# A branch for rare slots moved to the program's end, record reads freed of the scatters, and weights of the second layer requested from the last slot

## The chip, the core and the metric

The kernel runs on one core of a Trainium2 chip. Its time is device microseconds of one execution. TensorE (PE in the profile) does the matrix products, VectorE (DVE), ScalarE (ACT) and GpSimd (POOL) the element work, and SyncE (SP) issues most of the transfers. POOL issues the indirect transfers, which read or write rows by a list of indices. Each engine works through its own list of instructions in order, and waits for the others by semaphores.

## The reference

Three stages follow one another over 8 sequences of 576 tokens, 4608 tokens of 512 values in all:

```python
ret = scores * Dmat            # retention: causal, decaying, 8 heads of 64
x = (ret @ v)                  # 4608 x 512
logits = x @ w_gate + modality_bias[modality_id]
e_idx = argmax(logits); gate_w = softmax(logits)[e_idx]
out[mask] = gate_w[mask] * (relu(x[mask] @ w1[e]) @ w2[e])   # 8 experts, 512 -> 1024 -> 512
h = x @ w_in                   # second layer: 512 -> 2048
out = (relu(h) ** 2) @ w_out   # 2048 -> 512
```

Everything is fp32. Which expert a token goes to is known only when the kernel runs.

## The kernel before

**Retention and routing (0 to about 180 us).** 36 tiles of 128 tokens are computed by PE. The routing of a group of tiles gives every token a row in a table `perm`, sorted by expert. POOL writes these rows by indirect transfers (`perm<-gt,pi`, L467), one for 128 tokens, each with a small `spacer` instruction ahead of it (L464), which holds the transfer back until a given instruction of ACT, DVE or PE has run.

**The experts (about 180 to 611 us).** The sorted tokens are cut into slots of 512, each with the weights of one expert. Slot 0 is worked in two halves of 256 rows, slots 1 to 7 in two halves of 256 to 512 columns, and slot 8 has 384. For a half of slot 0, SP reads its records from `perm` (`records_rows`, L556), POOL turns the row numbers into integers (`rixr`, L558) and gathers the tokens by two indirect transfers (`xg<-xl,rixr`, L565). ACT and DVE copy them (`xn`, L571), PE transposes them (`tr`, L581) and multiplies: `hp` (first product, L615 to L617), `hh` and `hl` (the activated result on ACT and DVE, L620 and L621), `yp` (second product, L640). For the later slots the gather (`xg<-xl,rix`, L549) takes eight transfers a half, and DVE transposes (L597). Every fp32 operand is split into a high and a low part, so that a product is three matmuls. `craw`, `ca`, `cm` and `cw` (L802 to L825) prepare the weights of the second layer meanwhile: an integer addition on POOL (L807), two chains on ACT and DVE, and a transfer to memory.

**The order of this work is written out by hand.** The dictionary `OPT` holds for each slot the tick at which a step is put into the engines' lists: `e0` for slot 0 (`rec` the reading of the records, `g1` the gather of the second half, `xn1` its copies, `raw` the weight loads), `bs` for the later slots. Its entry `m2` gives the steps for the second layer that the last slot's ticks hold: `wl` requests a block of input weights (`wq_load`, `wqr<-cw`, L1037), `ws` forms its sums on POOL (`wq_sums`, L1043), `wh` splits it on ACT and DVE (`wq_split`), `xf`, `xs`, `xh` and `xp` do the like for the tokens, `ol` and `oh` for the output weights (`wor`). A framework adds the waits: by default a read of `perm` waits for every earlier write to it, and every later write waits for the read.

**Rare slots.** 9 slots always run (`NSURE`). Up to 7 more run if the experts' shares of the tokens need them: `with tc.If(st.hv > 0)` at L1336, between the last slot and the second layer. On these inputs it isn't taken; all engines then jump over its body.

**The second layer (about 611 to 1388 us).** 72 pairs `hquad(n)` (42 matmuls: seven products of the first layer for one block, `px`, `py` and `pr_all`, L1368 to L1370) and `zquad(n)` (24 matmuls of the second, `zp`, L1427 to L1430). PE's list has hquad 0, hquad 1, zquad 0, hquad 2, zquad 1 and so on. Between a quad's products ACT copies them out of PSUM into `mc` (L1378, L1381, L1385), POOL adds (L1382 to L1387), DVE adds and squares (L1390, L1391), ACT and DVE make the high and low parts `gh` (L1394) and `gl` (L1395) for the zquad. `mc` has one buffer. The lists `before`, `gaps`, `posts` and `tails` set at which quad the next weights and tokens are loaded and split. At the end POOL writes the rows of the result by indirect transfers (`out<-zo,ti`, L1444).

Of the kernel before, what the change touches and what calls it, by code (L numbers as in the profile page):

```python
# [77 lines left out]
def consts():  # L78
# [28 lines left out]
    sm[:, 228] = p // Q  # L107
    c["csta"] = np.concatenate([tri, gj, tabk.reshape(P, -1), tabs.reshape(P, -1)], 1).astype(np.float32)
# [16 lines left out]
OPT = dict(manual=True, nbig=10,nlate=10,nx=2,b0=2,bl='SG',rl=2,pz=5,ve=lambda m:'GV' if m<3 or m%4==0 else 'GS',vn=(4,4,2),egn=2,nps=2,npo=1,npt=2,npm=4,nwarm=11,ew=(20,25,32,33),es={23:1,24:1,25:1,26:1,28:1,29:1,30:1,31:1},rlag=1,rlagl=1,rlate=35,rperl=30,e5=5,e6=4,ld=4,rper=8,nw=3,biasat=4,keep=(5,0,4,2),nxw=3,scs=2,e3=13,ylag=2,zlag=2,gb=3,zb=4,cf=(0,6,7,12),cf0=(0,8,9,13),hv=10,zend=1,cwm={0:3},cws={i:(1 if i<4 else 2) for i in range(2,14)},cv0=8,scat=lambda i,n: 2,f3=33,f4=34,f5=34,e0=dict(ro=1,esplit={2:4,3:2,4:2},r1=0,r2=2,r3=2,tab=(7,8,8,9),rec=5,raw=(0,0,1,3),g1=7,split={5:2,6:2,7:2,8:3,9:3,10:2,11:2},xn1=11,tr0=6,tr1=4),hh=3,hl=3,ylag2=1,bs1=dict(regs=1,rec=1,raw=(3,4,5,6),g0=3,g1=7,gn0=(2,)*4,gn1=(2,)*4,split={6:1,7:1,8:2,9:2,10:1,11:2,12:2,13:1,14:2,15:2},tr0=10,tr1=13,cv=1),bs=dict(regs=-9,rec=-9,raw=(0,3,6,8),g0=-4,g1=4,gn0=(1,)*8,gn1=(1,)*8,split={3:1,4:2,6:1,7:1,8:2,9:3,10:2,11:1,12:2,14:1},tr0=5,tr1=13,cv=2,f0=7,p0=13,m2={1:('wl 0','xf'),4:('ws 0','xs 0'),5:('xh 0',),6:('wh 0 0',),7:('xs 1',),8:('xh 1',),9:('wh 0 1','wl 1','xs 2'),10:('xh 2','xp 1','ol 0'),11:('xp 4','ws 1'),12:('wh 1 0',),13:('wh 1 1',),14:('oh 0',),15:('oh 1',)}))  # L125


def kernel_body(tc, I, out):
# [90 lines left out]
    pq = small[:, 228:229]  # L219
    modi = cp.tile([P, NTILE, 2], I32, name="mod_c")  # L220
# [167 lines left out]
    st.fine = True  # L388

# [62 lines left out]
    def route3(gi):  # L452
# [5 lines left out]
        for i in range(n):  # L458
            def f(i=i):
# [9 lines left out]
                tc.add_to_no_dep_group("scat", sc.ins)  # L469
            soon.append((gi, f))  # L470
# [58 lines left out]

    def records(row, n):  # L530

        rec = sp.tile([P, 2, 8, 2], F32, name="rec", bufs=3)
        src = perm[ds(row, n * HW)].rearrange("(h i a) w -> h i (a w)", h=n, a=8)
        for h in range(n):
            nc.sync.dma_start(out=rec[:, h].rearrange("p a w -> p (a w)"), in_=bc(src[h], 0, 4))
        return rec
# [1005 lines left out]
```

## Time and profile before

| what | value |
|---|---|
| time, median of 3 runs | 1398.53 us (1396.82 to 1400.24) |
| profiled execution | 1399.43 us, its span 1397.6 us |
| PE busy | 1354.1 us, 97% of the span |
| DVE, POOL, ACT busy | 871.6, 537.2 and 519.4 us |
| granted TensorE clock, mean | 0.990 |
| transfers | 182.08 MB, mean 130 GB/s |

The profile shows one execution. A bracket behind an instruction is the time for which its engine stood idle ahead of it, and what it waited for last. [...] Busy shares over the whole span hide where PE stands: it has to be looked for stretch by stretch.

### The profile page before, as it was taken

How to read it: one execution, taken by the hardware profiler on the slowest of the kernel's cores; microseconds unless marked ns; L12 is line 12 of the kernel's file. 1: busy time of each engine (PE TensorE's matmuls, PEld its weight loads, DVE VectorE, ACT ScalarE, POOL GpSimd, SP SyncE). 2: the span in 40 equal slices, each digit the busy share in tenths (PEclk: the TensorE clock that was granted, in tenths of full speed). 3: DMA queues.
4: the chain of work that ended last, by engine and by line, in shares of the span. 5: the costliest groups of instructions: out<-in, count | busy, mean ns of one | idle time of the engine just before them, and what ended most of it. 6: DMA issues, size and time to landing. Idle time of an engine off the chain costs nothing.

```text
span 1397.6 us, 24821 instructions
## 1 busy us (share of the span) xinstructions
PE 1354.1 (97%) x9728; PEld 1187.9 (85%) x9728; DVE 871.6 (62%) x1320; ACT 519.4 (37%) x969; POOL 537.2 (38%) x675
## 2 busy tenths in 40 slices
PE   9999997999999999989999999999999999999996
PEld 7877787878888888988989989988988998998895
DVE  6667776698777877647455445454666655656542
ACT  2323353354443444334333333333433333333321
POOL 0123455454453535134322222235733344244332
PEclk9999998999999999999999999999999999999998
DMA  8799877467765667431111100113222222122210
GB/s 295 220 234 235 235 176 251 154 198 226 245 225 188 205 211 251 122 102 37 61 61 61 61 31 31 61 61 106 83 84 61 91 91 77 45 81 72 91 62 30
DMA packets 99243, 182.08 MB, mean 130 GB/s; under 512 B 25004, under 2 KB 43820, under 8 KB 94764
## 3 DMA queue, kind: packets, MB, share of 16 engines
q1 hardware_dynamic: 90412, 160.95, 37.9%
q0 software_dynamic: 8704, 19.45, 4.4%
q8 instruction: 78, 1.28, 0.4%
q14 instruction: 49, 0.40, 0.1%
HBM read 133.58 MB, written 46.77 MB: 129 GB/s over the span
## 4 chain that ended last, share of the span: by engine, by line
PE 53%; issue 1%; DMA 0%; POOL 0%; DVE 0%; SPq 0%; ACT 0%; POOLq 0%; DVEq 0%
PE zp L1428 9%; PE zp L1427 9%; PE zp L1430 9%; PE px L1370 5%; PE px L1369 5%; PE px L1368 5%; PE py L1368 2%; PE py L1370 2%; PE py L1369 2%; PE pr_all L1370 1%; PE pr_all L1368 1%; PE pr_all L1369 1%; DMA yraw<-yT 0%; POOL out L1444 0%; DVE wql L1017 0%
## 5 line engine op out<-in xcount | busy, mean ns | idle before, releaser
L1427 PE MATMUL zp<-woh,gh 128*128 128x512 f32 x576 | 227.9, 396 | 0.0
L1428 PE MATMUL zp<-wol,gh 128*128 128x512 f32 x576 | 227.5, 395 | 0.0
L1382 POOL TENSOR_TENSOR mc<-mc 128x256 f32<-128x256 f32 x72 | 56.3, 782 | 432.9 <-ACT mc L1381 432.8
L1390 DVE TENSOR_TENSOR mc<-px,mc 128x512 f32<-128x512 f32 x72 | 49.8, 691 | 260.8 <-POOL mc L1386 260.7
L549 POOL DMA_INDIRECT xg<-xl,rix x136 | 143.7, 1057 | 168.2 <-DVE rix L542 130.1
L1430 PE MATMUL zp<-woh,gl 128*128 128x512 f32 x576 | 166.2, 394 | 0.0
L1394 ACT CAST gh<-mc 128x1024 fp32r<-128x1024 f32 x72 | 75.5, 1049 | 239.9 <-DVE mc L1391 238.6
L1395 DVE TENSOR_TENSOR gl<-mc,gh 128x1024 fp32r<-128x1024 f32 x72 | 88.6, 1231 | 81.9 <-ACT gh L1394 81.9
L1430 PEld LDWEIGHTS zp<-woh,gl 128*128 128x128 f32 x576 | 108.4, 188 | 25.3
L1427 PEld LDWEIGHTS zp<-woh,gh 128*128 128x128 f32 x576 | 108.9, 189 | 22.3
L1428 PEld LDWEIGHTS zp<-wol,gh 128*128 128x128 f32 x576 | 109.0, 189 | 22.0
L1368 PE MATMUL px<-xq,wqh 128*128 128x256 f32 x432 | 123.0, 285 | 3.1 <-DVEq L1336 3.1
L1370 PE MATMUL px<-xq,wql 128*128 128x256 f32 x432 | 123.5, 286 | 2.6 <-DVE wql L1017 2.6
L640 PE MATMUL yp<-hh,whi 128*128 128x512 f32 (+2 forms) x352 | 123.3, 359 | 0.0
L1369 PE MATMUL px<-xq,wqh 128*128 128x256 f32 x432 | 123.1, 285 | 0.0
L640 PE MATMUL yp<-hh,wlo 128*128 128x512 f32 (+2 forms) x352 | 122.8, 357 | 0.0
L521 DVE TENSOR_TENSOR wlo<-raw,whi 128x512 fp32r<-128x512 f32 x160 | 107.5, 706 | 8.1 <-ACT whi L520 7.7
L1378 ACT COPY mc<-px 128x512 f32<-128x512 f32 x72 | 42.3, 587 | 174.5 <-PE px L1370 159.7
L620 ACT ACTIVATE hh<-hp 128x512 fp32r<-128x512 f32 (+2 forms) x88 | 46.6, 529 | 156.4 <-PE hp L617 153.9
L615 PE MATMUL hp<-xhi,whi 128*128 128x512 f32 (+1 forms) x256 | 98.9, 386 | 0.0
L616 PE MATMUL hp<-xlo,whi 128*128 128x512 f32 (+1 forms) x256 | 98.9, 386 | 0.0
L617 PE MATMUL hp<-xhi,wlo 128*128 128x512 f32 (+1 forms) x256 | 98.8, 386 | 0.0
(221 smaller groups left out, 3361.7 us busy)
## 6 DMA issues: line engine op xcount, KB each, us to landing
raw<-in_w SPq DMA_DIRECT2D x34, 1024.0 KB
kqv<-in_kqv SPq DMA_DIRECT2D x108, 256.0 KB
yraw<-yT SPq DMA_DIRECT2D x66, 256.0 KB
zA<-zo SPq DMA_DIRECT2D x36, 256.0 KB
zo<-zA SPq DMA_DIRECT2D x36, 256.0 KB
xl<-xr SPq DMA_DIRECT2D x34, 256.0 KB
craw<-in_wi SPq DMA_DIRECT2D x16, 512.0 KB
cw<-cm SPq DMA_DIRECT2D x32, 256.0 KB
```

Source lines behind the costliest of these rows:

```text
L521: V.tensor_tensor(out=lo[:, j], in0=raws[i][:, j], in1=hi[:, j].bitcast(F32), op=A.subtract)
L549: G.indirect_dma_start(out=g.x[:, a].rearrange("p k j -> p (k j)"), out_offset=None, in_=xl.rearrange("t (b e) -> (t b) e", b=4)[0:4 * P * ...
L615: PE.matmul(hp, w1h[:, kc, cs], xh[:, kc], start=(kc == 0), stop=False)
L616: PE.matmul(hp, w1h[:, kc, cs], xlo[:, kc], start=False, stop=False)
L617: PE.matmul(hp, w1l[:, kc, cs], xh[:, kc], start=False, stop=(kc == 3))
L640: PE.matmul(hf.yp[dd], w2[:, fb, dd * P:(dd + 1) * P], h, start=start and f == 0 and (w > HW or dd % 2 == 0), stop=stop and f == 7, skip_g ...
L1368: PE.matmul(o, w.hi[:, m, kc], hi[:, kc], start=start and kc == 0, stop=False, skip_group_check=True)
L1369: PE.matmul(o, w.hi[:, m, kc], lo[:, kc], start=False, stop=False, skip_group_check=True)
L1370: PE.matmul(o, w.lo[:, m, kc], hi[:, kc], start=False, stop=stop and kc == 1, skip_group_check=True)
L1427: PE.matmul(zps[s][j], at(gh, j), wh[:, fb], start=(p == 0 and f2 == 0), stop=False)
L1428: PE.matmul(zps[s][j], at(gh, j), wl[:, fb], start=False, stop=False)
L1430: PE.matmul(zps[s][j], at(gl, j), wh[:, fb], start=False, stop=(p == 3 and f2 == 1))
```

## The change

- The `If` goes to the program's end. Since the second layer has then been computed already, its body runs slots 1 to 8, the rare ones and the whole second layer once more, with a packed placement (`st.packed`); for that the routing tables get six further small DVE instructions, and the index of the result's rows (`x_index`) is masked by `st.all`.
- Reads of the records are put into a group of accesses that need not wait for one another with the scatters issued after them (`read_rows`, `recread`). The cast of the row numbers (`rixr`) moves from the record read to the gather. In `e0` the second half's records, gather and copies come two ticks earlier, one weight load one tick later; the scatters go on at one more tick.
- The last slot's ticks also request blocks 2 and 3 of the input weights (`wl 2`, `wl 3`), sum block 2 (`ws 2`; block 3 right after the slots) and fetch the next tokens (`xn`); in the second layer their splits come one quad earlier. The first quad's `mc` has a buffer of its own.

The diff, cut to its core:

```diff
-f4=34, e0=dict(rec=5, raw=(0,0,1,3), g1=7, xn1=11, ...)
+f4=35, e0=dict(rec=3, raw=(0,0,1,4), g1=5, xn1=9, ...)
-m2={..., 12:('wh 1 0',), ..., 15:('oh 1',)}
+m2={..., 12:('wh 1 0','wl 2'), ..., 15:('oh 1','ws 2','wl 3','xn')}
@@ route3
                 tc.add_to_no_dep_group("scat", sc.ins)
+                tc.declare_no_dep(sc.ins, group="recread", reason="...")
+    def read_rows(dst, src):
+        d = nc.sync.dma_start(out=dst, in_=src)
+        if scats or soon:
+            tc.add_to_no_dep_group("recread", d.ins)
@@ records_rows, gather_rows
-        nc.sync.dma_start(out=rec, in_=perm[ds(row, HW)].rearrange("(j p) w -> p j w", p=P))
+        read_rows(rec, perm[ds(row, HW)].rearrange("(j p) w -> p j w", p=P))
+        return rec
+
+    def gather_rows(rec, tiles=NTILE):
+
         ix = sp.tile([P, 2], I32, name="rixr", bufs=2)
         G.tensor_copy(out=ix, in_=rec[:, :, 1])
-        return ix
-
-    def gather_rows(ix, tiles=NTILE):
-
@@ tables
-        ci = place(r0, "c")
+        ci, cf, cd, rare = T("pic", [NSLOT], I32), pick(r0, "c"), lag, e8[:, 0:1]
+        V.tensor_tensor(out=cf, in0=cf, in1=pos, op=A.add)
+        V.tensor_scalar(out=rare, in0=SI[:, 7:8], scalar1=float(NSURE - 1), scalar2=None, op0=A.is_gt)
+        st.all = e8[:, 1:2]
+        V.tensor_scalar(out=st.all, in0=rare, scalar1=-1.0, scalar2=1.0, op0=A.mult, op1=A.add)
+        V.tensor_scalar(out=tokf, in0=tokf, scalar1=rare, scalar2=None, op0=A.mult)
+        V.tensor_tensor(out=cd, in0=spread, in1=cf, op=A.subtract)
+        V.scalar_tensor_tensor(out=ci, in0=cd, scalar=rare, in1=cf, op0=A.mult, op1=A.add)
+        packed = es_.bitcast(I32)
+        V.tensor_copy(out=packed, in_=cf)
@@ one tick of the half-slot
         if st.exs and st.exs.steps:
             gather_some(st.exs, o_.egn)
-        elif m != o_.f4:
+        else:
             scatter_some(o_.scat(m, len(scats)))
@@ after the slots
     while pending:
         ypart()
+    wq_sums(3)
+    esB.close()
@@ hquad
-        c = mp.tile([P, 4, HW], F32, name="mc")
+        c = mp.tile([P, 4, HW], F32, name="mc") if n else bigt("mc", F32, (P, 4, HW))
@@ the lists of the second layer
-    at(before, 0, wq_load, 2)
-    at(before, 0, x_fetch, 1)
-    at(before, 0, wq_load, 3)
     at(before, 0, wo_load, 1)
-    at(tails, 0, wq_sums, 2)
-    at(gaps, 1, wq_splits, 2)
-    at(tails, 1, wq_sums, 3)
-    at(gaps, 2, wq_splits, 3)
-    at(gaps, 2, run_los)
-    at(posts, 2, wo_splits, 1)
+        at(gaps, 0, wq_splits, 2)
+        at(gaps, 0, run_los)
+        at(gaps, 1, wq_splits, 3)
+        at(gaps, 2, wo_splits, 1)
@@ the end of the program
+    second_layer("oscat", ())
     with tc.If(st.hv > 0):
-        rare_slot(NSURE)
+        esB = contextlib.ExitStack()
+        first_pools(esB)
+        first_work(esB)
+        for s in range(1, NSURE + 1):
+            rare_slot(s)
         for s in range(NSURE + 1, NSLOT):
             with more(s):
                 rare_slot(s)
+        esB.close()
+        st.packed = True
+        m2 = [x.split() for _, xs in sorted(bs["m2"].items()) for x in xs]
+        second_layer("oscat2", [lambda x=x: M2[x[0]](*map(int, x[1:])) for x in m2] + [lambda: wq_sums(3)])
```

What follows is the order of instructions at three places, without times. First POOL's list around the gather for the first half of slot 0, before (`perm` is the table of scattered records, `xT` and `xlast` the tiles that the spacers wait for):

```order
L464 COPY spacer<-xT 128x1
L467 DMA perm<-gt,pi 37376x2
L558 CAST rixr<-recr 128x2
L461 CAST pi<-pf 128x6
L464 COPY spacer<-xT 128x1
L467 DMA perm<-gt,pi 37376x2
L464 COPY spacer<-xT 128x1
L467 DMA perm<-gt,pi 37376x2
L565 DMA xg<-xl,rixr 128x512 x2
L464 COPY spacer<-xlast 128x1
L467 DMA perm<-gt,pi 37376x2
```

and after the change:

```order
L467 COPY spacer<-xT 128x1
L470 DMA perm<-gt,pi 37376x2
L467 COPY spacer<-xT 128x1
L470 DMA perm<-gt,pi 37376x2
L467 COPY spacer<-xlast 128x1
L470 DMA perm<-gt,pi 37376x2
L467 COPY spacer<-xlast 128x1
L470 DMA perm<-gt,pi 37376x2
L571 CAST rixr<-recr 128x2
L574 DMA xg<-xl,rixr 128x512 x2
L467 COPY spacer<-xlast 128x1
L470 DMA perm<-gt,pi 37376x2
```

The cast `rixr`, which needs the records from memory, stood ahead of two scatters; now four scatters stand ahead of it, and eight rather than ten lie between this gather and the next.

Second, ACT's list at the end of the first half of slot 0, before (`xn` is the copy of the gathered second half, `cm` the first of the second layer's weight chains, which needs POOL's integer addition to `craw`):

```order
L520 CAST whi<-raw 128x512 x3
L620 ACTIVATE hh<-hp 128x256
L520 CAST whi<-raw 128x512 x3
L620 ACTIVATE hh<-hp 128x256
L653 COPY yo<-yp 128x256 x2
L520 CAST whi<-raw 128x512 x2
L814 ACTIVATE cm<-craw 128x512
L620 ACTIVATE hh<-hp 128x256
L520 CAST whi<-raw 128x512 x2
L571 COPY xn<-xg 128x512
```

and after:

```order
L524 CAST whi<-raw 128x512 x3
L629 ACTIVATE hh<-hp 128x256
L524 CAST whi<-raw 128x512 x3
L580 COPY xn<-xg 128x512
L629 ACTIVATE hh<-hp 128x256
L662 COPY yo<-yp 128x256 x2
L524 CAST whi<-raw 128x512 x2
L832 ACTIVATE cm<-craw 128x512
L629 ACTIVATE hh<-hp 128x256
L524 CAST whi<-raw 128x512 x2
```

The copy `xn` has moved from behind `cm` and its neighbours to a place ahead of the last `hh` of the first half.

Third, SP's list from the last slot's token store (`yT<-yo ... 384`) to the second layer, before; the body of the branch is left out between the two fences, of which the first is ahead of it:

```order
L1037 DMA wqr<-cw 128x512 x2
L1058 DMA wor<-cw 128x1024 x2
L794 TENSOR_LOAD t_hvi
L667 REGISTER_ALU
L667 DMA yT<-yo 512x1x384
L663 ISA
L663 DMA meta<-rec 32x16
L663 ISA
L663 DMA meta<-rec 16x16
L1336 COMPARE_AND_BRANCH
```

and behind it:

```order
L1336 UNCONDITIONAL_BRANCH
L1037 DMA wqr<-cw 128x512 x2
L1077 DMA yraw<-yT 128x2x256 x4
L1037 DMA wqr<-cw 128x512 x2
L1058 DMA wor<-cw 128x1024 x2
L1083 DMA mt<-meta 128x2x2 x2
```

After the change the same stretch reads:

```order
L1061 DMA wqr<-cw 128x512 x2
L1082 DMA wor<-cw 128x1024 x2
L812 TENSOR_LOAD t_hvi
L1061 DMA wqr<-cw 128x512 x4
L1101 DMA yraw<-yT 128x2x256 x4
L676 REGISTER_ALU
L676 DMA yT<-yo 512x1x384
L672 ISA
L672 DMA meta<-rec 32x16
L672 ISA
L672 DMA meta<-rec 16x16
L1082 DMA wor<-cw 128x1024 x2
L1107 DMA mt<-meta 128x2x2 x2
```

The requests for weight blocks 2 and 3 (`wqr`) and the next tokens (`yraw`) now stand ahead of the last slot's store, the branch is gone from here, and only the output weights (`wor`) are left behind the store.

## Rows read from the trace of the kernel before

**Rows 1.** Stretches: length, busy PE PEld DVE ACT POOL, PEclk, DMA share, GB/s.

```profile
223.70:228.50 4.80, 3.99 (x18) 3.70 (x19) 3.69 (x8) 1.42 (x3) 2.13 (x2) 0.50 0.40 114
613.90:617.40 3.50, 3.49 (x18) 3.49 (x19) 0.00 (x0) 0.59 (x1) 0.00 (x0) 0.56 0.43 150
627.20:631.20 4.00, 4.00 (x17) 3.61 (x18) 0.90 (x2) 2.48 (x5) 3.84 (x6) 0.60 0.99 351
638.80:641.60 2.80, 2.80 (x13) 2.80 (x14) 2.80 (x4) 0.30 (x1) 0.50 (x1) 0.50 0.00 0
660.00:1375.00 715.00, 715.00 (x4472) 644.43 (x4471) 385.41 (x461) 254.10 (x407) 264.50 (x354) 1.00 0.21 67
```

**Rows 2.** PE at slot 0: start, length, engine, line, operation, [idle before, releaser].

```profile
197.09 0.99 PE L581 MATMUL tr<-ident,xn 128*128 128x128 f32 x7 [0.42 <-DVE xn L571]
...
214.62 0.64 PE L640 MATMUL yp<-hl,whi 128*128 128x256 f32 x4
...
223.72 0.48 PE L581 MATMUL tr<-ident,xn 128*128 128x128 f32 x1 [8.46 <-ACT xn L571]
...
228.90 0.28 PE L640 MATMUL yp<-hh,whi 128*128 128x256 f32 x1
```

**Rows 3.** ACT, the first weight chain.

```profile
221.18 0.67 ACT L814 ACTIVATE cm<-craw 128x512 f32<-128x512 f32 x1 [10.18 <-POOL craw L807]
```

**Rows 4.** POOL from the first gather of slot 0 to slot 1's gathers.

```profile
180.63 0.19 POOL L558 CAST rixr<-recr 128x2 int32<-128x2 f32 x1 [10.05 <-DVE gt L436]
...
187.40 1.28 POOL L467 DMA_INDIRECT perm<-gt,pi  x1 [0.17 <-issue]
...
201.42 0.96 POOL L467 DMA_INDIRECT perm<-gt,pi  x1 [0.16 <-issue]
...
210.19 0.19 POOL L558 CAST rixr<-recr 128x2 int32<-128x2 f32 x1 [7.80 <-DMA recr<-perm]
...
212.34 1.27 POOL L565 DMA_INDIRECT xg<-xl,rixr  x1 [0.30 <-issue]
...
220.12 1.03 POOL L807 INT64_ADD craw<-craw  x1 [6.50 <-issue]
...
225.84 1.19 POOL L549 DMA_INDIRECT xg<-xl,rix  x1 [4.69 <-issue]
...
248.83 0.94 POOL L549 DMA_INDIRECT xg<-xl,rix  x1 [0.30 <-issue]
```

**Rows 5.** SP, the records of the second half.

```profile
208.31 0.38 SPq L556 DMA_DIRECT2D recr<-perm  x1
```

**Rows 6.** PE, the three waits at the start of the second layer.

```profile
613.91 0.39 PE L1368 MATMUL px<-xq,wqh 128*128 128x256 f32 x1 [3.15 <-DVEq L1336]
...
627.17 0.39 PE L1368 MATMUL px<-xm,wqh 128*128 128x256 f32 x1 [2.92 <-ACT mc L1378]
...
638.76 0.58 PE L1370 MATMUL px<-xq,wql 128*128 128x256 f32 x1 [2.56 <-DVE wql L1017]
```

**Rows 7.** POOL, the last scatter of the result.

```profile
1387.09 0.96 POOL L1444 DMA_INDIRECT out<-zo,ti  x1 [0.33 <-DVE zo L1442]
```

**Rows 8.** The page, its first line.

```profile
span 1397.6 us, 24821 instructions
```

**Rows 9.** Transfers, 176 to 216 us: gathers, count, median us to landing.

```profile
xg<-xl,rixr POOLq DMA_INDIRECT x4, 6.5
```

**Rows 10.** DVE: a table step, and slot 1's transposes of the second half.

```profile
211.59 0.29 DVE L768 TENSOR_REDUCE t_prc<-t_c 128x16 f32<-128x128 f32 x1
...
257.63 2.22 DVE L597 STREAM_TRANSPOSE xf<-xg 128x512 f32<-128x512 f32 x2
```

**Rows 11.** ACT in the first quad.

```profile
618.57 0.59 ACT L1381 COPY mc<-py 128x512 f32<-128x512 f32 x1 [1.44 <-PE py L1370]
...
623.74 1.05 ACT L1394 CAST gh<-mc 128x1024 fp32r<-128x1024 f32 x1 [4.02 <-DVE mc L1391]
```

**Rows 12.** DVE, the last copy of the last slot.

```profile
610.80 0.56 DVE L653 COPY yo<-yp 128x384 f32<-128x384 f32 x1 [0.49 <-PE yp L640]
```

More of the change, by code (lines that the diff above doesn't have):

```diff
@@ L469, in f @@
                 tc.add_to_no_dep_group("scat", sc.ins)
+                tc.declare_no_dep(sc.ins, group="recread", reason="the rows read were all written by groups before this one; every token has a row of its own")
             soon.append((gi, f))
@@ L1087, in x_index @@
         k.ti = sp.tile([P, 4], I32, name="ti", bufs=2)
-        V.tensor_copy(out=k.ti, in_=k.mt[:, :, 1])
+        g = 4 * GSEQ[n][1]
+        if st.packed:
+            V.tensor_copy(out=k.ti, in_=k.mt[:, :, 1])
+        else:
+            V.scalar_tensor_tensor(out=k.ti, in0=k.mt[:, :, 1], scalar=st.all, in1=tokf[:, g:g + 4], op0=A.mult, op1=A.add)
     XPART = ((0, 2), (3, 6), (5,))
@@ L1404, in z_back @@
-    def z_back(s):
-        zos[s] = [zb.tile([P, DM], F32, name="zo") for _ in range(4)]
-        for j in range(4):
-            nc.sync.dma_start(out=zos[s][j], in_=zA[GSEQ[s][1], j])
-    def zquad(n):
-        s, p = n // 4, n % 4
-        ph, g = GSEQ[s]
-        k = XS[8 if s == 9 else s]
-        if p == 0:
-            zps[s] = [ps_z.tile([P, DM], F32, name="zp", tag="zp") for _ in range(4)]
-        gh, gl = gs.pop(n)
-        wo = WO[2 * ph + p // 2]
-        wh, wl = wo.hi, wo.lo
-        end = n == nq - 1
-        def mms(f2, js):
-            fb = 2 * (p % 2) + f2
-            def at(g, j):
-                return g[:, SLOT[f2][j // 2], P * (j % 2):P * (j % 2 + 1)]
-            for j in js:
-                PE.matmul(zps[s][j], at(gh, j), wh[:, fb], start=(p == 0 and f2 == 0), stop=False)
-                PE.matmul(zps[s][j], at(gh, j), wl[:, fb], start=False, stop=False)
-            for j in js:
-                PE.matmul(zps[s][j], at(gl, j), wh[:, fb], start=False, stop=(p == 3 and f2 == 1))
-        def leave(j):
-            if ph == 0:
-                zo = zb.tile([P, DM], F32, name="zo")
-                if j % 2:
-                    V.tensor_scalar(out=zo, in0=zps[s][j], scalar1=k.mt[:, j, 0:1], scalar2=None, op0=A.mult)
-                else:
-                    SC.activation(out=zo, in_=zps[s][j], func=AF.Copy, scale=k.mt[:, j, 0:1])
-                nc.sync.dma_start(out=zA[g, j], in_=zo)
-                return
-            zo = zos[s][j]
-            V.scalar_tensor_tensor(out=zo, in0=zps[s][j], scalar=k.mt[:, j, 0:1], in1=zo, op0=A.mult, op1=A.add)
-            G.memset(spacer, 0.0)
-            sc = G.indirect_dma_start(out=out, out_offset=bass.IndirectOffsetOnAxis(ap=k.ti[:, j:j + 1], axis=0), in_=zo, in_offset=None)
-            tc.declare_no_dep(sc.ins, group="oscat", reason="every token has a row of its own")
-            tc.add_to_no_dep_group("oscat", sc.ins)
-        if p < 3:
-            for f2 in range(2):
-                mms(f2, range(4))
-        else:
-            if not end:
-                mms(0, range(4))
-            for j in range(4):
-                for f2 in range(2) if end else (1,):
-                    mms(f2, [j])
-                leave(j)
-        if s == 8 and p % 2:
-            drop(wh, wl)
@@ L1514, in kernel_body @@
-    for n in range(nq):
-        for fn in before.pop(n, ()):
-            fn()
-        run_los()
-        hquad(n, gaps.pop(n, ()), posts.pop(n, ()))
-        if n:
-            zquad(n - 1)
-        for fn in tails.pop(n, ()):
-            fn()
-    zquad(nq - 1)
-    assert not before and not gaps and not posts and not tails
-    esC.close()
+        esB.close()
+        st.packed = True
+        m2 = [x.split() for _, xs in sorted(bs["m2"].items()) for x in xs]
+        second_layer("oscat2", [lambda x=x: M2[x[0]](*map(int, x[1:])) for x in m2] + [lambda: wq_sums(3)])
```

307 lines of the change are left out of this document (193 added, 114 removed).

## The prediction

> **What bounds the kernel now.** I read first the page's busy shares, which say that PE is busy for 97% of the span. Such a kernel can be made shorter only where PE stands still or runs at its lower clock, so I then went through the span by stretches and looked for those. From 660 to 1375 us there is nothing to find: PE is busy for 715.00 of 715 us at a granted clock of 1.00 [rows 1]. Three places are left, and the change touches each.
>
> Place A, slot 0, the turn from its first to its second half. PE's last `yp` of the first half ends at 214.62 + 0.64 = 215.26. The next work, the transposes `tr`, starts at 223.72 after an idle time of 8.46 us put down to ACT's copy `xn`, and `yp` goes on at 228.90 [rows 2]. [...] Undisturbed, that work is eight transposes (0.99 us for seven, so 1.1 [rows 2]) and 12 matmuls at 0.11 (13 of this kind take 2.80 us at 0.50 [rows 1], so 0.22 there and half at full clock): 2.4 us. The place costs 228.90 - 215.26 - 2.4 = 11.2 us.
>
> What held `xn` up is read backwards. ACT stood for 10.18 us at `cm`, which is ahead of `xn` in its list, for POOL's integer addition [rows 3]; POOL began that at 220.12, 6.5 us after the second gather transfer (212.34 + 1.27 = 13.61) had been written out. POOL had waited 7.80 us for the records, at 210.19 [rows 4]; SP had asked for them at 208.31 [rows 5], which is 5.9 us after POOL's last scatter ended (201.42 + 0.96 = 202.38). And POOL was late with that scatter since it had stood 10.05 us at the cast `rixr` of the first half, with the scatters queued behind it [rows 4]. (That idle time names an old DVE instruction; the cast's input comes from the records.)
>
> Place B, the start of the second layer. PE waits three times: 3.15 us at the branch, 2.92 us for ACT's copy of quad 1 into the one buffer `mc`, which the first quad's `gl` still reads, and 2.56 us for the split of weight block 2 [rows 6], 8.63 us in all. After each the clock is low, with 0.56 over 3.5 us, 0.60 over 4.0 us and 0.50 over 2.8 us [rows 1]: 3.5 x 0.44 + 4.0 x 0.40 + 2.8 x 0.50 = 4.5 us of lost work. Together 13.2 us.
>
> Place C, the end. The last scatter of the result leaves POOL at 1387.09 + 0.96 = 1388.05 [rows 7]; the span ends at 1397.6 [rows 8]. These 9.5 us are its landing and the program's end.
>
> **The change part by part.** At A, four scatters stand ahead of the first half's cast rather than two, and they go in the 10 us in which POOL stood still. Eight scatters then follow the gather, where ten did. Those ten start from 187.40 to 201.42, one every 14.02 / 9 = 1.56 us [rows 4]. The cast may be as late as before, at 180.63, but two scatters no longer stand between it and its gather: cast and gather took 213.61 - 210.19 = 3.4 us at the second half, so the next scatter starts at about 184.6, and the last of eight at 184.6 + 7 x 1.56 = 195.5; it ends at 196.5, 5.9 us earlier than before. Records are asked for 5.9 us later (202.4), the cast follows after 1.9 (204.3), and the gather is written out after 3.4 (207.7). A gather lands 6.5 us after its issue [rows 9]; the last issue is near 206.5, so the landing is near 213, or a microsecond or two sooner if the scatters go through faster. The reading's new group takes no wait from the second half's records: it still needs every scatter.
>
> The copies `xn` now stand ahead of `cm`, so that the transposes no longer wait for the integer addition. In exchange ACT waits at `xn` from about 207 to 213, with the last `hh` of the first half queued behind it, and DVE with `hl`. PE wants those at 213.7 and 214.6, so this costs 0 to 1 us. The six added DVE steps, at up to 0.29 us each [rows 10] some 1.5 us, fall into DVE's wait for the same gather. The transposes follow at 215.3 to 216.3, and PE needs the next `hh` 2.4 us later. That one stands behind `cm`, and `cm` behind the addition. If the addition keeps its 6.5 us to the gather, it starts at 214 and ends at 215, and `hh` comes at 216.5; if it was really waiting for the weights that it adds to, a load that SP now issues behind another load of expert weights, it may start at 217, with `hh` at 219.5. PE goes on between 218 and 220.5: a gain of 8.4 to 11.
>
> Not all of it stays. Slot 1's gathers follow the addition (before at 225.84) and end at 249.77 [rows 4]; its second transposes start at 257.63 [rows 10], 7.9 us later, where 6.5 are needed for the landing. So that chain has 1.4 us of slack, and it moves forward only as the addition does, by 3 to 6 us. PE, ahead of it by more, will meet a new wait at slot 1's start: A is worth 4.4 to 7.4 by that chain, up to 11 if the landing is quicker than the median. I take 7.
>
> At B the first wait goes with the branch. PE's list has the first `px` directly behind the last `yp`, and block 0, block 1 and the first tokens are split before the slots end. Then PE runs hquad 0 and starts hquad 1. The second wait was for `mc`; it now has a buffer of its own, so quad 1's copy waits no more for `gl`, but it still stands behind `gh` of quad 0 in ACT's list. From ACT's copy of `py` to the end of `gh` it took 624.79 - 618.57 = 6.2 us [rows 11], and the copy of `px` takes 0.6 more. PE meanwhile has 18 matmuls of hquad 0 and 30 of hquad 1 to do, 48 at 0.11 us, or 5.3 us. A wait of 1.5 us is left. The third wait goes if block 2 is ready: it is requested ahead of the last slot's store rather than behind that and the branch, and its sums run on POOL while that has nothing else to do. Block 3 follows in the same way. What is pushed back is the last slot's store and its records, behind eight more loads, and the output weights `wor`. Neither is needed before zquad 2, which three hquads and two zquads precede. So B gives 13.2 - 1.5 = 11.7; with a low clock after the remaining wait (1.5 us lost, as after the other three) 10.2; and 13.2 at most.
>
> At C the branch comes back, once. Each engine compares and jumps over the body, waits there for the scatters where it has to, and jumps again to the program's end. The nearest row is the branch in the middle: DVE's last copy ended at 610.80 + 0.56 = 611.36 [rows 12] and PE's `px` started at 613.91, so 2.55 us passed for both jumps. The first jump lies beside the landing of the last scatters, the second behind it. Bounds: 0 if both are covered, 5 if each costs a full 2.5; I take 2. [...]
>
> The sum: -7 - 11.7 + 2 = -16.7 against the profiled execution's 1399.43, so 1382.7; that run lies 0.9 above the median of 1398.53, which gives 1381.8. I predict 1382.
>
> **The rivals.** First, the gain at A is given back almost whole by slot 1's gathers, or the second half's records come no earlier since the scatters are held by their landings and not by POOL. For it speaks the slack of only 1.4 us; against it that POOL stood idle for 10 us while scatters were ready. A is then 1 to 3: 1398.5 - 2 - 11.7 + 2 = 1387.
>
> Second, at B the third wait stays in another form. The splits of blocks 2 and 3 now stand in quads 0 and 1, ahead of `gh` and `gl` on ACT and DVE. If DVE's two steps for block 2 push `gl` behind zquad 0's need, PE waits there 2 to 3 us and its clock falls, at 1.5 more. B is then 7, and the time 1398.5 - 7 - 7 + 2 = 1386.5. Against it: block 2 is loaded while ACT and DVE wait for POOL's additions.
>
> Third, all is better than the middle: A 10, B 13, C 1, so 1376.5.
>
> Fourth, slower: the jump at the end is paid by the instructions that it skips, and serially. Before, 2.55 us went with 1369 skipped instructions of PE; now 7657 are skipped (both counted in PE's lists), which in proportion is 14.3 us, and the last jump begins only when the landing is over. Against the 18.7 us won at A and B it decides from 9.4 us for each of the two jumps; at 14.3 for each, partly beside the landing, the time would be about 1398.5 - 18.7 + 24 = 1404. Nothing in the profile speaks for a price that grows with the length, except that no second branch was taken to compare.
>
> That the change doesn't do what it says would be the case if the branch were taken: the counts exclude it, for the same inputs took none.
>
> **How the numbers follow.** The forecast as worked out (1378 to 1385) has a chance of 0.52, the first rival 0.20, the second 0.12, the third 0.11, the fourth 0.03, and 0.02 is left for no difference. A measurement of this kernel can tell 0.2%, some 2.8 us, from no change; all cases but the last two are faster by more. So faster 0.95, same 0.02, slower 0.03. The range from 1375 to 1389 takes in the first three rivals' middles and most of the unknown costs.
>
> **What would show it.** POOL's idle time at the first `rixr` shrinks from 10 us to little, and the second records are read near 202 us. PE's wait ahead of the second `tr` falls from 8.46 to about 1 us, and a new wait of 1 to 4 us appears by slot 1's transposes between 240 and 256 us. At the second layer the first `px` follows the last `yp` without a gap, one wait of 1 to 2 us is left in hquad 1, and none at block 2. From POOL's last scatter to the span's end it is 10 to 14 us rather than 9.5. I would be wrong if PE still stood at `tr` for over 4 us, if the start of the second layer kept two waits of over 2 us, or if the end grew by over 5 us.

## The result and the profile after

The changed kernel takes 1384.61 us (median of 4 runs, 1382.63 to 1387.14) against 1399.38 for the kernel before in the same comparison (4 runs, 1396.82 to 1402.52). The ratio is 0.9894, with a 95% interval of 0.9867 to 0.9922: 14.8 us faster, where 16.7 were forecast. The time lies in the range given.

The page of the changed kernel, its span and its busy shares:

```profile
span 1382.1 us, 24811 instructions
...
PE 1345.6 (97%) x9728; PEld 1180.6 (85%) x9728; DVE 872.7 (63%) x1326; ACT 519.4 (38%) x969; POOL 542.2 (39%) x675
```

The span was 1397.6 [rows 8]. PE runs as many matmuls as before, so the 15.5 us must come from stretches in which it stood or ran slowly. They are found by taking the start of the same matmul in both traces at a few marks and following how far the new trace is ahead. In us, minus is a gain:

| trace | start to 160 | 160-213 | slot 0's turn 213-240 | slot 1 240-300 | 300-600 | start of layer 2 600-660 | 660-1380 | end |
|---|---|---|---|---|---|---|---|---|
| after | -1.2 | +3.5 | -9.2 | +1.1 | 0 | -12.3 | -1.9 | +4.5 |
| forecast | 0 | 0 | -8.4 to -11 | +1 to +4 | 0 | -11.7 | 0 | +2 |

**Place A.** POOL around the two gathers of slot 0 in the timeline after (start, length, engine, line, operation, idle time before and what ended it), to be laid beside [rows 4]:

```profile
182.97 0.19 POOL L571 CAST rixr<-recr 128x2 int32<-128x2 f32 x1 [1.03 <-DMA recr<-perm]
...
197.72 1.37 POOL L470 DMA_INDIRECT perm<-gt,pi  x1 [0.16 <-issue]
...
206.12 0.63 POOL L571 CAST rixr<-recr 128x2 int32<-128x2 f32 x1 [7.04 <-DMA recr<-perm]
...
208.50 0.97 POOL L574 DMA_INDIRECT xg<-xl,rixr  x1 [0.30 <-issue]
...
218.50 1.93 POOL L825 INT64_ADD craw<-craw  x1 [9.04 <-DVE yo L662]
...
224.79 1.19 POOL L558 DMA_INDIRECT xg<-xl,rix  x1 [4.36 <-ACT hh L629]
```

The idle time at the first cast has fallen from 10.05 to 1.03 us, the last scatter starts at 197.72 instead of 201.42, and the second gather is out at 209.47 instead of 213.61. ACT and PE follow, to be laid beside [rows 2, 3]; two of ACT's rows, then three of PE's:

```profile
214.57 0.62 ACT L580 COPY xn<-xg 128x512 f32<-128x512 f32 x1 [5.12 <-DMA xg<-xl,rixr]
...
220.47 0.68 ACT L832 ACTIVATE cm<-craw 128x512 f32<-128x512 f32 x1 [3.42 <-POOL craw L825]
```

```profile
217.73 0.74 PE L649 MATMUL yp<-hl,whi 128*128 128x256 f32 x4 [0.69 <-DVE hl L630]
218.30 1.04 PE L590 MATMUL tr<-ident,xn 128*128 128x128 f32 x8
...
221.47 0.39 PE L649 MATMUL yp<-hh,whi 128*128 128x256 f32 x1 [0.72 <-ACT hh L629]
```

The transposes wait for the gather and not for the integer addition. The wait of 8.46 us has become three of under 0.8 (the third, 0.78 us, is at 234.33), and eight transposes take 1.04 us. By this point the trace has lost 2.3 us against the one before (-1.2 + 3.5 in the table), so times here are to be read 2.3 us earlier when they are laid beside the old rows.

**Place B.** PE at the start of the second layer, beside [rows 6]:

```profile
604.60 0.34 PE L649 MATMUL yp<-hl,whi 128*128 128x384 f32 x1
604.78 0.28 PE L1398 MATMUL px<-xq,wqh 128*128 128x256 f32 x1
...
614.59 0.39 PE L1398 MATMUL px<-xm,wqh 128*128 128x256 f32 x1 [1.07 <-ACT mc L1408]
```

The first `px` stands directly behind the last `yp`; of the three waits one of 1.07 us is left (1.5 were forecast). The stretches after it (length; busy PE, PEld, DVE, ACT, POOL; PEclk, DMA share, GB/s), beside [rows 1]:

```profile
614.60:618.20 3.60, 3.60 (x22) 3.22 (x23) 3.60 (x4) 2.99 (x5) 2.95 (x3) 1.00 0.44 147
...
660.00:1360.00 700.00, 700.00 (x4377) 630.61 (x4376) 380.55 (x454) 247.63 (x395) 262.24 (x351) 1.00 0.21 66
```

The granted clock (PEclk, as a share of full speed) stays at 1.00 behind a wait of 1.07 us, where it had been 0.50 to 0.60 behind waits of 2.56 to 3.15.

**Place C.** The last scatter of the result, beside [rows 7]:

```profile
1366.98 0.96 POOL L1474 DMA_INDIRECT out<-zo,ti  x1 [0.31 <-DVE zo L1472]
```

It ends at 1367.94, 14.2 us before the span does, instead of 9.5.

### The profile page after: what moved, and what is told of

The parts are those of the page before. It is cut to its first block, busy times and chain, and to the rows that moved or that the text cites. A ratio compares the mean times of both kernels' runs of the same rounds, so it can differ in the third digit from the quotient of the medians.

```text
span 1382.1 us, 24811 instructions
## 1 busy us (share of the span) xinstructions
PE 1345.6 (97%) x9728; PEld 1180.6 (85%) x9728; DVE 872.7 (63%) x1326; ACT 519.4 (38%) x969; POOL 542.2 (39%) x675
## 4 chain that ended last, share of the span: by engine, by line
PE 51%; issue 1%; POOL 1%; ACT 0%; POOLq 0%
PE zp L1460 9%; PE zp L1457 9%; PE zp L1458 9%; PE px L1398 5%; PE px L1400 5%; PE px L1399 5%; PE py L1398 2%; PE py L1399 2%; PE py L1400 2%; PE pr_all L1399 1%; PE pr_all L1400 1%; PE pr_all L1398 1%; POOL out L1474 0%; POOL mc L1416 0%; POOL mc L1412 0%
## 5 line engine op out<-in xcount | busy, mean ns | idle before, releaser
L1398 PE MATMUL px<-xq,wqh 128*128 128x256 f32 x432 | 121.7, 282 | 0.0
L1399 PE MATMUL px<-xq,wqh 128*128 128x256 f32 x432 | 121.5, 281 | 0.0
```

What stands on the lines that cost most here:

```text
L1398: PE.matmul(o, w.hi[:, m, kc], hi[:, kc], start=start and kc == 0, stop=False, skip_group_check=True)
L1399: PE.matmul(o, w.hi[:, m, kc], lo[:, kc], start=False, stop=False, skip_group_check=True)
```

## The experiments

Twelve runs in four sets. In each set the kernel before ran on the same chip; its median is given each time. Besides the medians, which scatter by some microseconds, I use the places of the table above.

**Set 1** asks what the branch costs at each of its two places, and what the slot 0 part gives (before: 1398.95).

*if_mid*: all of the change, but the branch stays between the slots and the second layer.

```diff
+    with tc.If(st.hv > 0):
+        rare_slot(NSURE)
+        ...
     esB.close()
     second_layer("oscat", ())
-    with tc.If(st.hv > 0): ...
```

> The changed kernel with the branch back between the slots and the second layer (its body the rare slots alone, as before); all else as changed. Theory: the branch costs about the same at either place. At the end the changed kernel has 4.5 us between POOL's last scatter and its final drain that the kernel before had not; in the middle PE waited 3.15 us and lost 1.5 us more at the low clock. So the time stays within 1 us of the changed kernel's 1384.6, the span's tail after the last scatter shrinks from 14.2 to 9.5 us, and PE gets a wait of about 3 us between the last yp and the first px. Rival (the forecast's own terms): the move is worth 4.7 - 2 = 2.7 us, so this one takes 1387.3. Second rival: with all weights loaded ahead the branch in the middle is covered, so this one is faster, 1380 to 1381.

1387.66 us, 0.9926 [0.9908, 0.9943]. My own view, a wash, fell; the time is the one that the rival gave (1387.3), but by luck, since both of its terms were too small. The start of the second layer gives -4.3 instead of -12.3, and the end costs -0.1 instead of +4.5. The branch in the middle costs 8.0 and not the 4.7 of its own wait, since the second wait comes back too, now at 4.09 us. PE, then ACT's first copy in this run and, last, the same copy in the kernel before:

```profile
604.00 0.39 PE L1397 MATMUL px<-xq,wqh 128*128 128x256 f32 x1 [3.10 <-DVEq L1557]
...
611.93 0.39 PE L1397 MATMUL px<-xm,wqh 128*128 128x256 f32 x1 [4.09 <-ACT mc L1407]
```

```profile
611.29 0.59 ACT L1407 COPY mc<-px 128x512 f32<-128x512 f32 x1 [10.39 <-SPq L1557]
```

```profile
616.54 0.59 ACT L1378 COPY mc<-px 128x512 f32<-128x512 f32 x1 [5.79 <-PE px L1370]
```

Here the copy waits for SP's part of the branch, which SP reaches only behind the last slot's store and records, and all of ACT's copies of the first quads start late. In the kernel before it was PE's product that ended its wait, and SP came to the branch only afterwards (617.40). So the 8.0 us hold a wait that the old branch did not cause, and what brought it in is not shown. Moving the branch is worth 8.0 - 4.5 = 3.5 us by the places, where the rival had 4.7 - 2 = 2.7.

*no_if*: the changed kernel without the branch and its body.

```diff
-    with tc.If(st.hv > 0):
-        ...
```

> The changed kernel without the branch: the rare slots are left out altogether, which these inputs do not need. Theory: POOL's final drain takes 8.7 us whatever stands ahead of it, and the 4.5 us of jump and semaphore work ahead of it are all serial; without the branch the tail after the last scatter is 9.5 us again and the time 1384.6 - 4.5 = 1380.1. Rival: the tail is the landing of the scatters, beside which the jumps lie; then the tail stays at 12 to 14 us and the time at 1383 to 1384.

1379.92 us, 0.9862 [0.9837, 0.9886], 4.5 to 4.7 us below the changed kernel, as the theory had it (1380.1). The last scatter ends 9.58 us before the span's end of 1380.6, as in the kernel before:

```profile
1370.06 0.96 POOL L1474 DMA_INDIRECT out<-zo,ti  x1 [0.31 <-DVE zo L1472]
```

*if_short_end*: the branch stays at the end, but its body holds only the rare slots.

```diff
-        for s in range(1, NSURE + 1):
-            rare_slot(s)
+        rare_slot(NSURE)
         for s in range(NSURE + 1, NSLOT): ...
-        st.packed = True
-        second_layer("oscat2", ...)
```

> The changed kernel with a short body in the branch at the end: it holds only the rare slots, and leaves out the repeated slots and second layer (not needed for these inputs). PE jumps over some 1370 instructions rather than 7657. If a jump has a price of its own, the tail stays at 14.2 us and the time at 1384.6, within 0.5. If the price grows with what is skipped, the 2.6 us from POOL's compare to its next semaphore shrink to under 1, the tail is 12 us and the time 1382.5.

1384.46 us, 0.9899 [0.9879, 0.9920], the changed kernel's time. The end costs +4.7 with 1370 skipped instructions of PE and +4.5 with 7657 (the body is cut for POOL as well, whose jump stands in the tail), so the price does not grow with the length. The last scatter, with a span of 1382.6:

```profile
1367.25 0.96 POOL L1474 DMA_INDIRECT out<-zo,ti  x1 [0.31 <-DVE zo L1472]
```

*slot0_old*: records, gathers and scatters of slot 0 as before, the rest as changed.

```diff
-f4=35, e0=dict(rec=3, raw=(0,0,1,4), g1=5, xn1=9, ...)
+f4=34, e0=dict(rec=5, raw=(0,0,1,3), g1=7, xn1=11, ...)
-                tc.declare_no_dep(sc.ins, group="recread", ...)
-            tc.add_to_no_dep_group("recread", d.ins)
-        else:
+        elif m != o_.f4:
             scatter_some(...)
```

> The changed kernel with slot 0 as before: the old ticks, record reads that wait, the row numbers' cast at the read, no scatters at the one tick. Second layer and branch as changed. By the traces PE gained 9.2 us at slot 0's turn and gave 2.8 us of it back by slot 1's end; the small loss of 3.4 us near 175 us is put down to chance. So this one should take 1384.6 + 6.4 = 1391.0, with PE's wait of about 8.5 us ahead of the transposes near 224 us back. Rival: the loss near 175 us is a price of the new order (POOL's two earlier scatters); then PE has no wait of over 1 us there in this kernel, and the time is 1387.6.

1388.40 us, 0.9926 [0.9906, 0.9945]: 3.8 us above the changed kernel, less than the 6.4 expected. The rival's 1387.6 is nearer, but its ground, a loss ahead of 213 us that comes with the new order, is refuted by after_again below. In the trace the old wait is back, 7.40 us ahead of the second half's transposes, and the places from 213 to 300 give -1.2 instead of -8.1. By the places it is worth about 7; the medians, from different comparisons, show 4.

```profile
223.73 0.47 PE L587 MATMUL tr<-ident,xn 128*128 128x128 f32 x1 [7.40 <-ACT xn L577]
```

**Set 2** takes the parts of A and B one by one. It ran on another chip (before: 1413.58). The trace of before, of an execution of 1399.43 us, is not from this chip, so up to 300 us these places mix chip and edit; from 300 us on they follow set 1's to 0.1 us.

*m2_old*: blocks 2 and 3 and the tokens requested after the slots, as before.

```diff
-m2={..., 12:('wh 1 0','wl 2'), ..., 15:('oh 1','ws 2','wl 3','xn')}
+m2={..., 12:('wh 1 0',), ..., 15:('oh 1',)}
-    wq_sums(3)
+    (loads, sums and splits in the second layer's lists as before)
```

> The changed kernel with the requests and sums of weight blocks 2 and 3 and the fetch of the next tokens back in the second layer, as before; branch at the end and the first quad's own buffer stay. Theory: of the 11.8 us won at the second layer's start 4.7 went with the branch, 3.4 with the buffer (2.92 + 1.6 less the 1.07 that is left) and 4.0 with the early requests (2.56 + 1.4). So this one takes 1384.6 + 4.0 = 1388.6, with a PE wait of 2 to 3 us for the split of block 2 in quad 2. Rival: the three waits hid each other, and with the two others gone this one grows; then PE waits 6 us or more there and the time is 1392 or more. Second rival: without the branch the requests come early enough; PE waits under 1 us, 1385.

1411.17 us, 0.9987 [0.9968, 1.0006]. The start of the second layer gives -4.3, so the early requests are worth 8.0; the theory that they are worth their old wait and its clock (4.0) fell, and the rival that this wait grows without the two others was right. PE now waits longer at block 2 than it ever did, and the stretch after it runs at 0.61:

```profile
640.75 0.58 PE L1399 MATMUL px<-xq,wql 128*128 128x256 f32 x1 [6.34 <-DVE wql L1041]
```

```profile
640.70:645.00 4.30, 4.25 (x23) 4.25 (x24) 4.30 (x6) 0.59 (x1) 0.59 (x1) 0.61 0.00 0
```

*mc_old*: the first quad's `mc` shares the one buffer again.

```diff
-        c = mp.tile([P, 4, HW], F32, name="mc") if n else bigt("mc", F32, (P, 4, HW))
+        c = mp.tile([P, 4, HW], F32, name="mc")
```

> The changed kernel with the first quad's products in the one shared buffer, as before. Theory: quad 1's copy on ACT waits again for DVE's low part of quad 0; PE's wait in hquad 1 grows from 1.07 to about 3 us and the clock falls after it, so 1384.6 + 3.4 = 1388.0. Rival: the copy is held by ACT's list anyway (it stands behind the high part of quad 0), and the buffer is worth 1.2 us or less: 1384.6 to 1385.8.

1406.95 us, 0.9954 [0.9935, 0.9972]. The place gives -7.7, so the buffer is worth 4.6, more than the theory's 3.4 and far from the rival's 1.2: the wait in hquad 1 is 3.28 us again, and the clock after it is 0.50.

```profile
630.93 0.58 PE L1398 MATMUL px<-xm,wqh 128*128 128x256 f32 x1 [3.28 <-ACT mc L1408]
```

```profile
631.00:635.00 4.00, 4.00 (x16) 3.71 (x17) 1.35 (x3) 3.88 (x7) 2.89 (x4) 0.50 0.00 0
```

Both medians lie further behind the changed kernel's ratio than these places say: 0.0093 x 1414 = 13 us where m2_old's start and steady part explain 9.9, and 8.5 where mc_old's explain 5.2. The missing 3 us lie within the intervals of the ratios. They could also come from slot 1, which takes back 5.3 and 8.0 us in these two traces of an unaltered slot 0, instead of 1.1. That would leave A 0.5 to 4.6 here, about as its first rival has it; but no trace of the kernel before was taken on this chip, so what the chip itself costs in that stretch is not known, and this is not shown.

*ticks_old*: only slot 0's ticks as before, with no scatters at the one tick. *rec_waits*: only the group of record reads taken out, so that the scatters behind a read wait for it again.

```diff
 ticks_old:
-f4=35, e0=dict(rec=3, raw=(0,0,1,4), g1=5, xn1=9, ...)
+f4=34, e0=dict(rec=5, raw=(0,0,1,3), g1=7, xn1=11, ...)
-        else:
+        elif m != o_.f4:
             scatter_some(...)
 rec_waits:
-                tc.declare_no_dep(sc.ins, group="recread", ...)
-            tc.add_to_no_dep_group("recread", d.ins)
```

> The changed kernel with the old ticks of slot 0 (records, gather, copies, weight load, and no scatters at the one tick), but with the freed record reads and the cast at the gather. Theory: the ticks carry the gain, since they put the copies ahead of the integer addition; the first half's cast then still holds POOL only until its records land. PE's wait ahead of the transposes is 5 to 8 us, and the time is 1389 to 1391. Rival: the freed reads and the moved cast carry it, as they bring all scatters forward; then the wait is under 3 us and the time 1385 to 1387.

> The changed kernel with record reads that wait as by default (and make later scatters wait for them); ticks and the place of the cast as changed. Theory: the scatters behind the first half's read wait for its landing, so POOL stands some 8 us ahead of 181 us as before, the last scatter comes about 3 us later, and so does the gather that PE waits for at slot 0's turn: a PE wait of 2 to 4 us there, time 1386.5 to 1388. Rival: the waits add nothing, since the scatters after the read are held by the spacers until the tile they wait for, about 177 us; then POOL's order of times is as in the changed kernel and the time 1384 to 1385.5.

1403.27 us (0.9912 [0.9888, 0.9935]) and 1405.13 us (0.9946 [0.9926, 0.9967]), so 2.5 and 7.4 us behind the changed kernel's ratio. From 160 to 300 us together the two traces stand at +8.2 and +6.7, where m2_old and mc_old, with slot 0 as changed, have +0.3 and +1.8 on the same chip. By the traces, the loss without either half is 5 to 8 us, for ticks_old more than its median bears out; its executions lie between 1395 and 1406, and the traced one is the slowest. In slot 0's turn ticks_old keeps -3.0 where the others have -8 to -10, and its trace has a wait of 6.08 us at 202 us that no theory had, for a step of the routing; its cause is not settled.

```profile
202.23 0.17 PE L451 MATMUL pr_all<-ohf,uprb 128*128 128x16 bf16 x1 [6.08 <-DVE ohf L425]
```

rec_waits keeps the turn (-10.1) and loses further up, +10.8 in 160-213 against +4.9 and +2.3 in m2_old and mc_old: the scatter behind the read of the first half's records waits 9.74 us on POOL for that read to land, the cast and the gather of the first half follow only behind it and further scatters, and PE stands at the first half's transposes.

```profile
190.72 0.98 POOL L470 DMA_INDIRECT perm<-gt,pi  x1 [9.74 <-DMA recr<-perm]
```

```profile
213.04 0.47 PE L587 MATMUL tr<-ident,xn 128*128 128x128 f32 x1 [4.90 <-ACT xn L577]
```

So the freed reads and the ticks belong together: the ticks alone move the wait from the second half to the first. The theory had POOL's wait, but PE's at the second half; the rival had none.

**Set 3** runs the changed kernel once more and tries to win something from a stretch that the forecast had left open: the first integer addition starts 6.5 us after the gather ahead of it on POOL [rows 4], and 9.0 us after it in the changed kernel (before: 1393.64).

*after_again* is the changed kernel unaltered. *warm_int* does a small integer addition early, on 8 values; *cv3* puts slot 1's weight chain two ticks later, behind that slot's gathers.

```diff
 warm_int, after the decays:
+    wint = bigt("wint", I32, (P, 4, 512))
+    G.memset(wint[:, 0, :8], 0)
+    G.int64_add(wint[:, 0, :8].bitcast(I64), wint[:, 0, :8].bitcast(I64), 1 << 28)
+    drop(wint)
 cv3:
-bs1=dict(..., cv=1)
+bs1=dict(..., cv=3)
```

> The changed kernel itself, unaltered, for two questions. The loss of 3.4 us near 175 us: chance, if this trace has anything between -1 and +4 there against the kernel before. The losses of up to 9 us at slot 1 in the traces of the second set of kernels, which hold the same slot 0: a matter of the chip they ran on, if this trace shows 2 us on a chip whose kernel before takes 1399, or 6 to 9 us where that takes 1413. Time: 0.9894 of the kernel before, within 0.003.

> The changed kernel with one small integer addition on POOL at the program's start. Theory: POOL's first integer addition (218.50, 9.0 us after the last gather transfer, with the DMA engines idle from 216 to 218) is late by a set-up that comes with the first instruction of its kind; with that made at the start it begins when its weights land, 214 to 215.5, slot 1's gathers begin 3 to 4 us earlier, and PE's give-back of 1.95 us at slot 1 goes: 1382 to 1383 where the changed kernel takes 1384.6. Rival: it waits for the landing of its weights, which comes at 218.4; then nothing moves, 1384.6.

> The changed kernel with the first weight chain (integer addition, cm, ca) two ticks later, behind slot 1's first two gather transfers. Theory: slot 1's gathers depend on the addition only by POOL's and DVE's lists; behind the move they begin at 214 to 217 rather than 224.8, the give-back of 1.95 us at slot 1 goes, and so do PE's three waits of 0.7 us for the hh behind cm: 2.5 to 4 us faster than the changed kernel. Rival: slot 1 is held by something else (its weights, or DVE's transposes in their place in the list), and the gathers' lead buys nothing: within 1 us of the changed kernel.

after_again: 1380.30 us, 0.9897 [0.9877, 0.9918], so the result repeats to 0.0003. Its places are those of after to 0.7 us, but for 160-213: -0.5 instead of +3.5. Six traces with the same code of slot 0 (after, after_again, if_mid, no_if, if_short_end, warm_int) lie between -0.5 and +3.5 there; that loss belongs to the run and not to the change.

warm_int: 1379.61 us, 0.9898 [0.9877, 0.9918], no gain. The theory's set-up is there: the addition starts 4.36 us after the gather where after_again, on the same chip, has 8.58. But slot 1's gathers, which the theory had 3 to 4 us earlier, stay where they were (221.03 in after_again), since their index `rix` comes from DVE, and only at 219.76. POOL in after_again, then POOL and DVE in warm_int:

```profile
214.62 1.03 POOL L825 INT64_ADD craw<-craw  x1 [8.58 <-DVE yo L662]
...
221.03 1.19 POOL L558 DMA_INDIRECT xg<-xl,rix  x1 [5.38 <-issue]
```

```profile
204.89 0.96 POOL L574 DMA_INDIRECT xg<-xl,rixr  x1 [0.30 <-issue]
...
210.21 1.04 POOL L825 INT64_ADD craw<-craw  x1 [4.36 <-DVE t_c L776]
...
220.73 0.95 POOL L558 DMA_INDIRECT xg<-xl,rix  x1 [9.48 <-issue]
```

```profile
219.76 0.23 DVE L551 TENSOR_SCALAR rix<-rec,cst_c 128x8 int32<-128x8 f32 x1
```

cv3: 1393.86 us, 0.9995 [0.9985, 1.0006]; all of A is lost, and more (+1.4 and +3.3 at the two places). The addition's set-up has moved with it, between two gathers of slot 1, and ACT's `cm` waits for the addition with `hh` queued behind it. POOL, ACT, and PE's waits from 196 to 270 us (total, times, longest):

```profile
219.51 0.95 POOL L558 DMA_INDIRECT xg<-xl,rix  x1 [0.30 <-issue]
...
230.11 1.03 POOL L825 INT64_ADD craw<-craw  x1 [9.65 <-issue]
```

```profile
231.18 0.67 ACT L832 ACTIVATE cm<-craw 128x512 f32<-128x512 f32 x1 [14.40 <-POOL craw L825]
```

```profile
PE yp L649 <- ACT hh L629: 10.1, 2, 9.3
```

**Set 4**, *warm_cv3*, is both edits together (before: 1393.68).

> The changed kernel with both: one small integer addition at the program's start, and the first weight chain two ticks later. Theory: the later chain alone lost 11 us at slot 0's turn only because the set-up of the first integer addition (9.65 us in that trace, 230.11 - 220.46) then stood between slot 1's gathers; with the set-up made at the start those 11 us come back, and the gathers, now ahead of the addition, start near 218 instead of 221, so that the 2 us given back at slot 1 go as well: PE's time from slot 0's second half to the end of slot 1 is 10 us shorter than in the kernel before rather than 8.4, and the whole 1.5 to 2 us shorter than the changed kernel (ratio 0.988 to the kernel before). Rival: the later chain is harmful by its place (its integer additions stand elsewhere among the gathers, and ACT and DVE meet them later); then this one is slower than the changed kernel by 2 us or more.

1383.88 us, 0.9927 [0.9914, 0.9941]. Without the set-up the addition follows the gather at once, and slot 0's turn is back at -9.2; but slot 1 costs +3.6 instead of +1.2. The result is the rival's, that the later place of the chain is harmful by itself. It ran alone on its chip, though, and slot 1 differed by more than that in set 2, so the cause is likely and not shown.

```profile
223.26 0.94 POOL L558 DMA_INDIRECT xg<-xl,rix  x1 [0.30 <-issue]
224.24 1.06 POOL L825 INT64_ADD craw<-craw  x1
```

No version with all of the work was clearly faster than the changed kernel.

## Why the prediction was right, step by step

**The direction and the sum.** -7 - 11.7 + 2 = -16.7 was forecast; by the places they are (-9.2 + 1.1) - 12.3 + 4.5 = -15.9, to which a part that nobody had forecast adds -1.9 (660-1380), and chance took 2.3 back ahead of 213 us. That the sum fits so well is in part luck: C came out 2.5 too dear, and A with 1.1, B with 0.6 and the 1.9 more than made up for it. Undoing each part alone gave back its own place and little else (slot0_old, if_mid; m2_old and mc_old from 300 us on).

**A: right, and for its reasons.** The cast stood ahead of the scatters; it no longer does. After the forecast's times (cast 204.3, gather out 207.7, landing near 213) the trace has 206.12, 209.47 and 214.5, all 1.5 to 1.8 late, in a trace that had lost 2.3 by then. PE resumed at 221.5, so at 219.2 without the 2.3, inside the 218 to 220.5. The give-back was sized too high. The step said that slot 1's chain has 1.4 us of slack and that PE would meet a wait of 1 to 4 us there. The gathers moved forward as forecast (225.84 to 224.79, with the 2.3 lost by then 3.3 us, of 3 to 6), and yet slot 1 cost only 1.1, and PE's only wait of over 0.1 us from 240 to 256 us is 0.79 us, for ACT's `hh` and not for the gathers. The step was wrong in the slack: it took 6.5 us for the landing, the median of slot 0's four gathers [rows 9], where slot 1's sixteen landed in 2.7 us in the same trace (222 to 256 us). The step had allowed for that only as its upper end:

```profile
xg<-xl,rix POOLq DMA_INDIRECT x16, 2.7
```

With its give-back A is worth 8.1 rather than 7. The first rival, A at 1 to 3, does not hold in the traces of after, set 1 and set 3; in those of set 2 slot 1 is dearer, and whether by the chip or by the change stays open.

**B: right.** 11.7 forecast, 12.3 measured: one wait of 1.07 us is left, and the clock does not fall behind it. The second rival's wait of 2 to 3 us at zquad 0 did not come: the only other wait up to 660 us is 0.35. That it is the early requests and the buffer that do it, each, is shown by m2_old and mc_old. What the sum of this term hid is that the three waits are not three prices: undone alone, the branch costs 8.0, the requests 8.0 and the buffer 4.6, 20.6 together, where all three are worth 12.3. For the requests the trace shows why: without the other waits PE is at block 2 sooner, and waits 6.34 us for it rather than 2.56. The branch's 8.0 is in part ACT's new wait for SP (if_mid), and mc_old's wait is nearly the old one.

**C: the term that was mis-sized.** I took 2 between 0 and 5, supposing that the first jump lies beside the landing of the last scatters. Measured are 4.5 (after), 4.7 (if_short_end) and 5.2 (after_again), and -0.1 without the branch (no_if). POOL's instructions at the end show why; first before, then after (start, length or end, in us; the queue's own instructions are not in the views of the profile):

```
before  1387.09  DMA_INDIRECT, last scatter   to 1388.05
        1386.85  DRAIN                        to 1396.78
after   1366.75  COMPARE_BRANCH
        1366.98  DMA_INDIRECT, last scatter   to 1367.94
        1369.61  semaphore events
        1370.13  INC_SWDGE_SEM                to 1372.44
        1372.48  DRAIN                        to 1381.21
```

The drain ends 1396.78 - 1388.05 = 8.7 us after the last scatter before, and takes 8.73 us after the change, but begins 4.5 us after the scatter. What I had called the landing is POOL's own drain, which begins its 8.7 us only when the jump and the semaphore work are over; nothing covers them. The landing itself is short, some 1.4 us in both traces, and lay beside the drain before and beside the jump after (there the DMA share is 0.54, at 203 GB/s, from 1367.94 to 1369.35 us, and 0.02 from 1369.35 to 1372.50). The stretches show it (length; busy engines; PEclk, DMA share, GB/s): behind the scatter before, in the drain before, and in the drain after. From 1389.50 us before, and from 1372.50 after, no transfer is left.

```profile
1388.05:1389.45 1.40, 0.00 (x0) 0.00 (x0) 0.00 (x0) 0.00 (x0) 0.00 (x0) 0.90 0.50 187
1389.50:1396.80 7.30, 0.00 (x0) 0.00 (x0) 0.00 (x0) 0.00 (x0) 0.00 (x0) 0.50 0.00 0
```

```profile
1372.50:1381.20 8.70, 0.00 (x0) 0.00 (x0) 0.00 (x0) 0.00 (x0) 0.00 (x0) 0.50 0.00 0
```

**The fourth rival** is refuted: the end costs +4.7 us with 1370 skipped instructions and +4.5 with 7657. Of the 4.5 us behind the scatter, 1.7 pass before POOL's first semaphore event (1367.94 to 1369.61) and 2.9 on the semaphore work up to the drain (to 1372.48); what the 1.7 go to, no run here shows.

**What stays open**: the 1.9 us in the steady second layer. PE is busy for 700.00 of 700 us there at a clock of 1.00 in both, yet the same matmuls come closer together: the distances differ by a few ns either way, and their sum is 1.9 us less, all of it after 1020 us. It goes with the build (-1.9 in every trace with the early requests and the own buffer, -0.03 in m2_old, -1.4 in mc_old); why, no run tells.

## What to carry to other kernels

Price waits that stand close together by undoing them one at a time in the new kernel, not by their length in the old one: here three waits worth 12.3 us together cost 8.0, 8.0 and 4.6 alone, since one had been partly covered by the others, and one held up another engine in the new order. An instruction that needs a round trip through memory belongs behind everything on its queue that is already ready: here POOL's idle time at the first cast fell from 10.05 to 1.03 us. And before a cost is booked as hidden behind the program's last transfer, look at what the queue itself does after that transfer: in both traces the last 8.7 us of this drain came only after the queue's other work (from 1388.05 before, from 1372.48 after), and hid nothing ahead of them.

## What the hardware showed unexpectedly

- The first integer addition on POOL has a set-up of its own: it starts 6.5 us after the gather in the kernel before, 9.0 in the changed one (8.58 in after_again) and 9.65 in cv3, but 4.36 (warm_int) and at once (0.04, warm_cv3) when a small addition has been done earlier. In cv3 it moved with the addition to the later place; there, where ACT's `hh` was queued behind the work that needs the addition, PE waited 10.1 us in two waits.
- POOL's drain at the end lasts 8.7 us beyond what precedes it, the last scatter in before (1388.05 to 1396.78) and the semaphore work in after (1372.48 to 1381.21); no transfer runs in its last 7.3 and 8.7 us. From the last scatter's end to the span's it is 9.5 us in before and 9.58 in no_if, 14.2 in after and 14.4 in if_short_end.
- One and the same stretch of 53 us ahead of slot 0's turn differed by up to 4.0 us between traces of the same code; a part worth 7 us had to be read from its place, not from one run's total.
